# Attention into an MLP on one core: a two-chunk first load, another order of jobs among the first tiles, and one pair of row copies on another engine

## The chip, the cores and the metric

The kernel runs on one core of a Trainium2 chip. The metric is the device time of one execution in microseconds (us), as a median of several runs. TensorE does matrix products, VectorE (DVE) and ScalarE (ACT) the elementwise work, GpSimd (POOL) and SyncE (SP) mostly issue DMAs here. SBUF is the memory on the core, and PSUM holds the results of TensorE in banks.

## The reference

Attention with a sigmoid in the place of the softmax, for 8 batches of 12 heads, then a two-layer MLP with a silu over all 3584 tokens. Inputs and output are float32.

```python
batch, n_heads, seq, head_dim = (8, 12, 448, 64)
scale = 1.0 / np.sqrt(q.shape[-1])
scores = scale * np.matmul(q, k.transpose(0, 1, 3, 2)) - np.log(S)
attn = 1.0 / (1.0 + np.exp(-scores))
attn_out = np.matmul(attn, v).astype(np.float32)
x = np.ascontiguousarray(attn_out.transpose(0, 2, 1, 3)).reshape(B * S, H * D)
# n_tokens, d_model, d_ff = (3584, 768, 2048)
h = x @ w_in
g = h * (1.0 / (1.0 + np.exp(-h)))
return (g @ w_out).astype(np.float32)
```

## The kernel before, in words

The 96 pairs of batch and head are taken in 24 quads of four heads, three quads to a batch. A quad has its 448 rows in seven chunks of 64, and a tile is one chunk of k of one quad: `scores` (L169) multiplies it with q (four matmuls, L178, into `psc`, of which there are two), and ScalarE takes the sigmoid of 896 columns into `attnT` (L185). `values` (L195) multiplies `attnT` with v (L209, into `pav`), and VectorE scales the sum into `xT` (L225), two copies for a quad. `ptr`, `pav`, `ph`, `pw` and `po` share four PSUM banks (`ps_1`).

q and k have to be transposed first. For quads 0 to 5 TensorE does this against an identity (`pe_transpose`, L139, 14 matmuls for q or k at L147), and VectorE copies the result, in two pieces of 512 and 384 columns, to `kT` or `qT` (L154). For quads 6 and up (`dma_transpose`, L158) an engine first brings the rows into another order (the "row copies", L162, `kr` and `qr`; L137 where ScalarE does it), and then SP issues a DMA that transposes (L163). `rows_of_quad` (L646) calls that, and after q it makes GpSimd wait for the transpose and then issues the next loads; behind q of quad 6 these are v of quad 6, k and q of quad 8, v of quad 7, then k and q of quad 9.

The order on every engine is the order in which the program is written; nothing is rescheduled. It has two stages that matter here.

The first 24 tiles (three quads of batch 0 and three tiles of batch 1) are written out one after another. Behind the scores of tile n stand the jobs that a table `behind` (L690) gives: transposes of later quads, rounds of `values`, or dummy products that only keep TensorE busy (`keep_busy(n, short)`, L131: n of 512 columns, `short` of 128). `unread` (L172) puts dummy products of 128 columns ahead of a tile's scores, in its own `psc`. k of quad 0 is loaded in two pieces (L596 and L597), of which the first has `FIRST` chunks. Only that first piece is transposed ahead of tile 0.

Then the MLP begins. For batches 0 and 1 `h_unit` (L238) makes one of 16 parts of h with six matmuls (L244, into `ph`), one for each pair of heads; pairs 0 to 3 come from quads 0 and 1, pairs 4 and 5 from quad 2. ScalarE takes the sigmoid (`tsig`, L256) and VectorE multiplies into `gTr` (L257), after which the bank is free. All of this is one long generator (`all_moe`, L559), each step of which stands for one matmul and gives its length in ns. Bursts of two tiles (L735) are set between stretches of its steps: one for each `PACE` = 1600 ns up to tile 42, then a stretch of 13500 ns, then bursts spread so that the steps up to `h_at` last until the batches' end. Two parts of h (`early`, L525) can be begun ahead of the stretches, and their steps there aren't counted.

Row copies of quads 6, 7 and 8 stand in `rows_at` (L524), by the number of the part of h after which they come, and ScalarE does them. Those of later quads stand in a list `later`; `rows_if_any` (L656) takes one behind each burst, and VectorE does it. Later stages (output products `po` at L465, and the h of later batches) are not changed.

Of the kernel before, what the change touches and what calls it, by code (L numbers as in the profile page):

```python
# [18 lines left out]
def kernel(  # L19
# [16 lines left out]
    NCH = S // HP  # L36
# [3 lines left out]
    NCC = DMODEL // P  # L40
    NFC = DFF // P
# [44 lines left out]
                rows_in(name, g)[:, :, c0 * D : c1 * D],  # L86
            )

    FIRST, SPLIT = 1, 4

    def load_first_q():
        room = cpool.tile([P, NHC * NO2 // 2], F32, tag="T2", name="qs")
# [76 lines left out]
    def scores(g, ch, unread=0):  # L169
        attnT[g, ch] = p12.tile([P, 2, S], F16, tag="attnT", name="attnT")  # L170
        psc = ps_sc.tile([P, 2, 512], F32, tag="pssc", name="psc")
        for _ in range(unread):  # L172
            nc.tensor.matmul(psc[:, 0, :P], dummy[:, :P], dummy[:, :P], start=True, stop=True)
        for half in range(2):
            own = slice(half * HP, (half + 1) * HP)
            for j in range(2):
                rows = slice(j * D, (j + 1) * D)
                nc.tensor.matmul(  # L178
                    psc[own, j, :S],
                    qkT["k", g][rows, ch, own],  # L180
                    qkT["q", g][rows, :, own],
                    start=True,
                    stop=True,
                )
        nc.scalar.activation(  # L185
            attnT[g, ch], psc[:, :, :S], AF.Sigmoid, bias=NEG_LOG_S, scale=QKSCALE
        )
# [50 lines left out]
    def h_unit(b, fc):  # L238
        nonlocal hold
        hold = b > 0 and fc == NFC - 1  # L240
        ph = ps_1.tile([P, 512], F32, tag="ps1", name="ph")
        for at, cc in enumerate(pairs):
            assert b in ready or at < 4
            nc.tensor.matmul(  # L244
                ph[:, :S],
                w_in_of[:, cc // NQ, cc % NQ, fc * P : (fc + 1) * P],
                xT[b][:, cc, :],
                start=(at == 0),
                stop=(at == NCC - 1),
            )  # L250
            if at < NCC - 1:
                yield 189
        if fc == NFC - 1:
            h_done.add(b)
        tsig = p3.tile([P, 2 * S], F16, tag="m1", name="tsig")[:, :S]
        nc.scalar.activation(tsig, ph[:, :S], AF.Sigmoid, bias=0.0, scale=ISX)  # L256
        nc.vector.tensor_mul(  # L257
            gTr[:, fc, (b % 2) * S : (b % 2) * S + S], ph[:, :S], tsig
        )
        yield 189  # L260
# [43 lines left out]
    def h_pair(m, tail):  # L304
# [56 lines left out]
        EARLY = NHC - 2  # L361
        behind = None
        yield from begin(0)
        for i in range(NHC):
            end = i == NHC - 1
            if not end:
                yield from begin(i + 1)
# [153 lines left out]
        yield 163  # L521


    rows_at = {14: (6, "k"), 16: (6, "q"), 18: (7, "k"), 21: (7, "q"), 27: (8, "k"), 30: (8, "q")}  # L524
    early = [h_unit(0, fc) for fc in range(2)]  # L525
    sums = w_sums()
    in_sums = w_in_sums()
# [57 lines left out]
    def stretch(ns):  # L585
        nonlocal done, due
        due += ns
        while done < due or hold:
            step_ns = next(stream, None)
            if step_ns is None:  # L590
                break
            done += step_ns
# [19 lines left out]
    units = [(g, ch) for g in range(NQB) for ch in range(NCH)]  # L612
# [30 lines left out]
    later = []  # L643
# [12 lines left out]
    def rows_if_any():  # L656
        if later:
            rows_of_quad(*later.pop(0), nc.vector.tensor_copy)

    def values_if_any():  # L660
        if not waiting:
            return 0
        g, begin, end = waiting.pop(0)
        rounds(g, end)
        return end - begin
# [10 lines left out]
    def transposes(g, name):  # L676
        pe_transpose(g, ((name, 0, 4), (name, 4, NCH)))
        if name == "q":
            after_transpose(g)
# [3 lines left out]
        if end == NCH:  # L683
            after_values(g)

    def begin(fc, steps):
        for _ in range(steps):
            next(early[fc])

    behind = {  # L690
        0: ((pe_transpose, 0, (("k", FIRST, 4),)),),
        1: ((pe_transpose, 0, (("k", 4, NCH),)), (after_transpose, 0)),
        2: ((keep_busy, 2),),
        3: ((transposes, 1, "k"),),
        4: ((transposes, 1, "q"),),
        5: ((keep_busy, 2),),
        6: ((keep_busy, 2),),
        7: ((keep_busy, 2),),
        8: ((transposes, 2, "k"),),
        9: ((transposes, 2, "q"),),  # L700
        10: ((rounds, 0, 2),),
# [1 line left out]
        12: ((rounds, 0, 7),),  # L703
        13: ((rounds, 1, 2),),
        14: ((rounds, 1, 4),),
        15: ((transposes, 3, "k"),),
        16: ((rounds, 1, 7),),
        17: ((transposes, 3, "q"),),
        18: ((rounds, 2, 3),),
        19: ((transposes, 4, "k"),),  # L710
        20: ((rounds, 2, 5),),
        21: ((transposes, 4, "q"),),
        22: ((rounds, 2, 7),),
        23: ((begin, 0, 3),),
    }
    for n in range(NT_B + 3):
        scores(*units[n], unread={0: 7, 1: 7, 2: 3}.get(n, 0))
        for do, *what in behind.get(n, ()):
            do(*what)

    PACE, BURST, ROUND, SPARE = 1600, 590, 200, 2400
    sets = 7 * NHC * 163
    h_at = [(2 * NFC * NCC - 3) * 189 + 3 * sets]
    for m in (1, 2):
        h_at.append(h_at[-1] + 7 * NHC * HCC * 189 + (3 + m % 2) * sets)
    AHEAD = 4
# [3 lines left out]
    for n in range(NT_B + 3, len(units), 2):  # L730
        burst = units[n : n + 2]
        if n == 2 * NT_B:
            values_if_any()
            stretch(13500)
        for u in burst:  # L735
            scores(*u)
        had = values_if_any()
        rows_if_any()
        for g, ch in burst:
            if ch == NCH - 3 and g >= 6 and g % 6 < 4 and g + 3 < NQB:  # L740
                later.extend(((g + 3, "k"), (g + 3, "q")))
            if ch == NCH - 1:
                waiting.extend(((g, 0, NCH),) if n < 2 * NT_B else ((g, 0, 4), (g, 4, NCH)))
        if n in (30, 32):
            transposes(5, "kq"[n // 2 - 15])
        if n < ends[0]:
            stretch(PACE)
            continue
        m = bisect.bisect(ends, n)
        if n + 2 == ends[m]:  # L750
            nc.scalar.activation(warm, warm, AF.Silu)
        dense = h_at[m - 1] - SPARE - done
        due = done
        stretch((dense + values_left * ROUND) / ((ends[m] - n) // 2) - had * ROUND)
        values_left -= had
        if n + 2 == ends[m]:
            while waiting:
                values_if_any()
                stretch(SPARE / 3)
            values_left = 2 * NT_B  # L760
            while 2 * m not in h_done:
                done += next(stream)
            due = done
            stretch(3000)
# [32 lines left out]
```

## Time and profile before

| | us |
|---|---|
| median of three runs | 368.06 |
| lowest, highest | 367.29, 368.47 |
| profiled execution | 367.27 |
| its span, first to last instruction | 365.5 |
| TensorE busy in it | 357.7 (98%) |
| VectorE, ScalarE, GpSimd busy | 263.4, 250.5, 63.1 |

The profile is one execution, and the views are of that one. A row of an order in time has its start and length in us, the engine, the line, the operation, what is written and read, and the count of instructions merged; in brackets the idle time ahead of it and what ended it. A row of a grouped view has the busy time in us and the mean in ns of one behind the bar. TensorE's matmuls overlap, so a row of one matmul is longer than its share of the time.

### The profile page before, as it was taken

The numbers are of one execution on the slowest core, as the hardware profiler recorded it, in microseconds if no ns is written. First come the engines' busy times: TensorE is split into PE (matmuls) and PEld (weight loads), VectorE is DVE, ScalarE is ACT, GpSimd is POOL, SyncE is SP. The second block draws the span as 40 slices with busy tenths as digits, with TensorE's granted clock in tenths as the row PEclk, the third lists the DMA queues.
The fourth block names the chain that finished last, engine by engine and source line by source line (L and its number), as shares of the span: only waits on it lengthen the run. The fifth ranks groups of instructions, "written<-read, shape, count | busy, mean of one in ns | idle before, by whom it ended". The sixth has DMA issues, their size and how long they took to land.

```text
span 365.5 us, 7663 instructions
## 1 busy us (share of the span) xinstructions
PE 357.7 (98%) x3027; PEld 181.0 (50%) x3027; DVE 263.4 (72%) x495; ACT 250.5 (69%) x364; POOL 63.1 (17%) x105
## 2 busy tenths in 40 slices
PE   7999999999999999999999999999999999999995
PEld 3554445444444555554444455554444455555662
DVE  2584779876888587877668677886867577778773
ACT  4998877797778677586677768658878756660000
POOL 8544300604241002002014001100100000000000
PEclk9999999999999999999999999999999999999999
DMA  8999999999999437307999653822844020003333
GB/s 131 198 205 205 205 204 187 168 160 163 202 158 211 91 89 102 50 0 141 153 194 166 142 112 56 108 40 47 169 78 112 17 70 0 3 0 88 86 86 86
DMA packets 65314, 42.78 MB, mean 117 GB/s; under 512 B 35968, under 2 KB 61824, under 8 KB 65280
## 3 DMA queue, kind: packets, MB, share of 16 engines
q0 software_dynamic: 26944, 22.58, 42.2%
q1 hardware_dynamic: 38112, 19.41, 25.7%
q8 instruction: 23, 0.38, 0.4%
q10 hardware_dynamic: 224, 0.33, 0.3%
q14 instruction: 11, 0.09, 0.1%
HBM read 45.61 MB, written 11.01 MB: 155 GB/s over the span
## 4 chain that ended last, share of the span: by engine, by line
PE 84%; issue 5%; ACT 4%; DMA 3%; DVE 2%; POOL 1%; ACTq 0%; POOLq 0%; DVEq 0%
PE po L465 36%; PE hy L320 11%; PE psc L178 10%; PE pav L209 8%; PE hz L320 7%; PE hx L320 7%; PE ph L244 5%; ACT attnT L185 4%; DMA kf<-in_k_dram 3%; DVE xs L273 1%; DVE xT L225 1%; DVE kT L154 0%; DVE osb L475 0%; POOL vf L84 0%; PE ptrk L147 0%
## 5 line engine op out<-in xcount | busy, mean ns | idle before, releaser
L185 ACT ACTIVATE attnT<-psc 128x896 f16<-128x896 f32 x168 | 144.3, 917 | 31.9 <-PE psc L178 31.3
L465 PEld LDWEIGHTS <-S 128*128 128x128 f16 x448 | 41.1, 98 | 36.4 <-issue 11.7
L178 PE MATMUL psc<-qT,kT 64*64 64x448 f16 x672 | 51.1, 363 | 1.1 <-ACT attnT L185 0.7
L475 DVE SCALAR_TENSOR_TENSOR osb<-po,osb 128x384 f32<-128x384 f32 x70 | 37.6, 554 | 19.4 <-PE po L465 18.8
L225 DVE TENSOR_SCALAR xT<-pav 128x448 f16<-128x448 f32 x45 | 26.1, 620 | 26.5 <-PE pav L209 26.4
L331 ACT ACTIVATE gTr<-u 128x448 f16<-128x448 f32 x48 | 27.6, 575 | 23.1 <-DVE u L344 19.1
L465 PE MATMUL po<-T,S 128*128 128x384 f16 x224 | 41.6, 327 | 0.0
L465 PE MATMUL po<-w_out_sb,S 128*128 128x384 f16 x224 | 41.5, 327 | 0.0
L320 PEld LDWEIGHTS <-w_in_sb 128*128 128x128 f16 x288 | 28.2, 98 | 26.4 <-issue 0.4
L209 PE MATMUL pav<-attnT,vf 64*64 64x448 f16 x672 | 41.0, 350 | 0.2
L465 PEld LDWEIGHTS <-gTr 128*128 128x128 f16 x304 | 28.0, 98 | 25.5 <-issue 8.5
L244 PE MATMUL ph<-xT,w_in_sb 128*128 128x448 f16 x192 | 38.9, 353 | 0.0
L465 PE MATMUL po<-w_out_sb,gTr 128*128 128x384 f16 x192 | 36.6, 327 | 0.0
L320 PE MATMUL hy<-xs,w_in_sb 128*128 128x448 f16 x144 | 35.1, 352 | 0.1
L320 PE MATMUL hx<-xT,w_in_sb 128*128 128x448 f16 x144 | 34.6, 352 | 0.0
L178 PEld LDWEIGHTS <-kT 64*64 64x64 f16 x672 | 16.0, 104 | 30.3 <-issue 27.1
L320 PEld LDWEIGHTS <-W 128*128 128x128 f16 x216 | 21.1, 98 | 19.6
L257 DVE TENSOR_TENSOR gTr<-ph,tsig 128x448 f16<-128x448 f32 x32 | 19.9, 623 | 11.0 <-ACT tsig L256 10.5
L84 POOL DMA_DIRECT2D vf<-in_v_dram x24 | 17.0, 713 | 61.2 <-PE pav L209 50.6
L244 PEld LDWEIGHTS <-w_in_sb 128*128 128x128 f16 x192 | 17.6, 98 | 19.1 <-issue 4.0
L475 DVE SCALAR_TENSOR_TENSOR osb<-po,m 128x384 f32<-128x384 f32 x42 | 23.0, 553 | 5.3 <-PE psc L178 2.0
L209 PEld LDWEIGHTS <-vf 64*64 64x64 f16 x672 | 20.3, 107 | 11.8 <-issue 2.0
(75 smaller groups left out, 416.8 us busy)
## 6 DMA issues: line engine op xcount, KB each, us to landing
out_dram<-osb SPq DMA_DIRECT2D x54, 192.0 KB, 3.0
vf<-in_v_dram POOLq DMA_DIRECT2D x24, 224.0 KB, 7.1
kf<-in_k_dram POOLq DMA_DIRECT2D x23, 224.0 KB, 5.8
qf<-in_q_dram POOLq DMA_DIRECT2D x23, 224.0 KB, 6.5
w_in_sb<-in_moe_w_in_dram POOLq DMA_DIRECT2D x8, 384.0 KB, 12.2
w_out_sb<-in_moe_w_out_dram POOLq DMA_DIRECT2D x4, 768.0 KB, 17.4
kT<-kr SPq DMA_TRANSPOSE x18, 4.6
qT<-qr SPq DMA_TRANSPOSE x18, 3.3
```

Source lines behind the costliest of these rows:

```text
L84: nc.gpsimd.dma_start(flat[name, g][:, :, c0:c1].rearrange("p j c d -> p j (c d)"), rows_in(name, g)[:, :, c0 * D : c1 * D],)
L178: nc.tensor.matmul(psc[own, j, :S], qkT["k", g][rows, ch, own], qkT["q", g][rows, :, own], start=True, stop=True,)
L185: nc.scalar.activation(attnT[g, ch], psc[:, :, :S], AF.Sigmoid, bias=NEG_LOG_S, scale=QKSCALE)
L209: nc.tensor.matmul(pav[half][j * D : (j + 1) * D, :S], flat["v", g][own, j, ch, :], at[own, j, :], start=(ch == 0), stop=(ch == NCH - 1),)
L225: nc.vector.tensor_scalar_mul(xT[b][:, half * NQ + iq, :], pav[half][:, :S], SX)
L244: nc.tensor.matmul(ph[:, :S], w_in_of[:, cc // NQ, cc % NQ, fc * P : (fc + 1) * P], xT[b][:, cc, :], start=(at == 0), stop=(at == NCC - 1),)
L257: nc.vector.tensor_mul(gTr[:, fc, (b % 2) * S : (b % 2) * S + S], ph[:, :S], tsig)
L273: nc.vector.tensor_sub(o, x, y)
L320: nc.tensor.matmul(ps, a[:, c, i * P : (i + 1) * P], bs(c), start=(first and c == 0), stop=(c == HCC - 1), skip_group_check=True,)
L331: nc.scalar.activation(gTr[:, side * NHC + i, odd * S : (odd + 1) * S], src, AF.Silu, scale=ISX)
L465: nc.tensor.matmul(po[:, :NO2], a[:, fc, :], w[:, fc, :], start=(fc == 0), stop=(fc == NHC - 1))
L475: nc.vector.scalar_tensor_tensor(out=o, in0=po, scalar=sign * scale, in1=x, op0=ALU.mult, op1=ALU.add)
```

## The change

- `FIRST` goes from 1 to 2: the first piece of k has two chunks, and so have the transposes and ScalarE's copy ahead of tile 0. Tile 1 needs no further transposes.
- The table `behind` is laid out anew: the rest of k of quad 0 comes behind tile 1 in two pieces, one dummy product stands behind tile 0, and tiles 2 and 5 to 7 have a long and a short dummy product instead of two long ones. The rounds of values and the transposes of quads 3 and 4 change places so that tile 17 has no job and the last round of quad 2 stands behind tile 23. `unread` is 7, 0, 5 for tiles 0, 1, 2 instead of 7, 7, 3.
- Eight steps of h (four of each of the first two parts, of pairs 0 to 3) come behind that, where there were three of the first part; `h_at` is set to match.
- The row copies of quad 8 leave `rows_at`; they go into `later` ahead of the burst of tile 42, so VectorE does them, k behind that burst and q behind the next.

```diff
-    FIRST, SPLIT = 1, 4
+    FIRST, SPLIT = 2, 4
...
-    rows_at = {14: (6, "k"), 16: (6, "q"), 18: (7, "k"), 21: (7, "q"), 27: (8, "k"), 30: (8, "q")}
+    rows_at = {14: (6, "k"), 16: (6, "q"), 18: (7, "k"), 21: (7, "q")}
...
-    def begin(fc, steps):
-        for _ in range(steps):
-            next(early[fc])
-
     behind = {
-        0: ((pe_transpose, 0, (("k", FIRST, 4),)),),
-        1: ((pe_transpose, 0, (("k", 4, NCH),)), (after_transpose, 0)),
-        2: ((keep_busy, 2),),
+        0: ((keep_busy, 1),),
+        1: ((pe_transpose, 0, (("k", FIRST, 4), ("k", 4, NCH))), (after_transpose, 0)),
+        2: ((keep_busy, 1, 1),),
         3: ((transposes, 1, "k"),),
         4: ((transposes, 1, "q"),),
-        5: ((keep_busy, 2),),
-        6: ((keep_busy, 2),),
-        7: ((keep_busy, 2),),
+        5: ((keep_busy, 1, 1),),
+        6: ((keep_busy, 1, 1),),
+        7: ((keep_busy, 1, 1),),
         8: ((transposes, 2, "k"),),
         9: ((transposes, 2, "q"),),
         10: ((rounds, 0, 2),),
...
         14: ((rounds, 1, 4),),
-        15: ((transposes, 3, "k"),),
-        16: ((rounds, 1, 7),),
-        17: ((transposes, 3, "q"),),
-        18: ((rounds, 2, 3),),
-        19: ((transposes, 4, "k"),),
-        20: ((rounds, 2, 5),),
-        21: ((transposes, 4, "q"),),
-        22: ((rounds, 2, 7),),
-        23: ((begin, 0, 3),),
+        15: ((rounds, 1, 7),),
+        16: ((transposes, 3, "k"),),
+        18: ((transposes, 3, "q"),),
+        19: ((rounds, 2, 3),),
+        20: ((transposes, 4, "k"),),
+        21: ((rounds, 2, 5),),
+        22: ((transposes, 4, "q"),),
+        23: ((rounds, 2, 7),),
     }
     for n in range(NT_B + 3):
-        scores(*units[n], unread={0: 7, 1: 7, 2: 3}.get(n, 0))
+        scores(*units[n], unread={0: 7, 2: 5}.get(n, 0))
         for do, *what in behind.get(n, ()):
             do(*what)
+    for unit in early:
+        for _ in range(4):
+            next(unit)
...
-    h_at = [(2 * NFC * NCC - 3) * 189 + 3 * sets]
+    h_at = [(2 * NFC * NCC - 8) * 189 + 3 * sets]
...
             stretch(13500)
+            later.extend(((8, "k"), (8, "q")))
         for u in burst:
             scores(*u)
```

## The prediction

> **What bounds the kernel now.** I read the busy shares first, then the stretches, then the orders in time of TensorE and ScalarE, since a share of 98% hides what kind of work fills it.
>
> ```profile
> PE 357.7 (98%) x3027; PEld 181.0 (50%) x3027; DVE 263.4 (72%) x495; ACT 250.5 (69%) x364; POOL 63.1 (17%) x105
> ```
> ```profile
> 10.00:15.00 5.00, 5.00 (x76) 2.28 (x72) 2.50 (x5) 5.00 (x7) 2.75 (x4) 1.00 1.25 201
> 60.00:80.00 20.00, 19.34 (x124) 9.14 (x121) 17.34 (x34) 16.31 (x26) 5.84 (x10) 1.00 1.21 170
> ```
>
> TensorE is the bound of the whole, so the time is its useful work plus what it wastes. In a row of stretches the columns after the length are PE, PEld, DVE, ACT, POOL, then the granted clock and the DMA share. From 10 to 15 us TensorE and ScalarE are both busy for all 5.00 us, yet part of TensorE's work there is dummy products. From 60 to 80 us 0.66 us is missing from TensorE. These are the two places that the change touches; the rest is dense and moves bodily. The first 29 us in TensorE's order in time (start, length, count at the end of the row):
>
> ```profile
> 1.46 3.25 PE L134 MATMUL pw<-dummy 128*128 128x512 f16 x10 [1.46 <-DVE warm L607]
> ...
> 5.27 0.22 PE L147 MATMUL ptrk<-ident,kf 128*64 128x128 f16 x2
> ...
> 6.32 0.38 PE L178 MATMUL psc<-qT,kT 64*64 64x448 f16 x4 [0.16 <-ACT qT L137]
> 7.01 0.36 PE L147 MATMUL ptrk<-ident,kf 128*64 128x128 f16 x6 [0.30 <-DMA kf<-in_k_dram]
> ...
> 8.02 0.38 PE L178 MATMUL psc<-qT,kT 64*64 64x448 f16 x4 [0.16 <-DVE kT L154]
> ...
> 11.40 0.38 PE L178 MATMUL psc<-qT,kT 64*64 64x448 f16 x4
> 11.71 0.61 PE L134 MATMUL pw<-dummy 128*128 128x512 f16 x2
> 12.25 0.38 PE L178 MATMUL psc<-qT,kT 64*64 64x448 f16 x4
> ...
> 14.78 0.38 PE L178 MATMUL psc<-qT,kT 64*64 64x448 f16 x4
> 15.09 0.58 PE L147 MATMUL ptrq<-ident,qf 128*64 128x128 f16 x14
> 15.60 0.38 PE L178 MATMUL psc<-qT,kT 64*64 64x448 f16 x4
> ...
> 25.58 0.56 PE L209 MATMUL pav<-attnT,vf 64*64 64x448 f16 x8
> 26.18 0.38 PE L178 MATMUL psc<-qT,kT 64*64 64x448 f16 x4
> 26.50 2.56 PE L244 MATMUL ph<-xT,w_in_sb 128*128 128x448 f16 x12
> 28.99 0.57 PE L178 MATMUL psc<-qT,kT 64*64 64x448 f16 x8
> ...
> 63.83 3.95 PE L244 MATMUL ph<-xT,w_in_sb 128*128 128x448 f16 x20
> ```
> ```profile
> 5.54 0.28 ACT L137 ACTIVATE kT<-ptrk 128x128 f16<-128x128 f32 x1 [0.63 <-PE ptrk L147]
> 5.71 0.48 ACT L137 ACTIVATE qT<-ptrq 128x384 f16<-128x384 f32 x1
> 6.75 0.92 ACT L185 ACTIVATE attnT<-psc 128x896 f16<-128x896 f32 x1 [0.56 <-PE psc L178]
> 8.46 19.30 ACT L185 ACTIVATE attnT<-psc 128x896 f16<-128x896 f32 x23 [0.79 <-PE psc L178]
> ...
> 29.54 1.72 ACT L185 ACTIVATE attnT<-psc 128x896 f16<-128x896 f32 x2
> ```
>
> Three things are to be seen. The sigmoid of tile 0 starts at 6.75, that of tile 1 only at 8.46: its scores (8.02) waited for chunk 1 of k. The 23 sigmoids that follow take 19.30 us, (19.30 - 0.92)/22 = 0.835 us from start to start, where two with nothing between them take 1.72 - 0.92 = 0.80; so TensorE, not ScalarE, sets part of the pace. A slot with two dummy products lasts 12.25 - 11.40 = 0.85 us, one with 14 transposes 15.60 - 14.78 = 0.82. And the twelve h matmuls at 26.50 take 2.56 us where (3.95 - 0.35)/19 = 0.19 us each (from the row of twenty) makes 2.44: 0.12 us is a hidden wait for the xT copies of quad 2.
>
> The second place, 67 to 74 us, TensorE and then ScalarE:
>
> ```profile
> 67.70 0.57 PE L178 MATMUL psc<-qT,kT 64*64 64x448 f16 x8
> 68.21 2.06 PE L244 MATMUL ph<-xT,w_in_sb 128*128 128x448 f16 x10
> 70.20 0.57 PE L178 MATMUL psc<-qT,kT 64*64 64x448 f16 x8
> 70.71 2.07 PE L244 MATMUL ph<-xT,w_in_sb 128*128 128x448 f16 x10
> 73.01 0.38 PE L178 MATMUL psc<-qT,kT 64*64 64x448 f16 x4 [0.24 <-ACT attnT L185]
> ...
> 74.13 0.36 PE L244 MATMUL ph<-xT,w_in_sb 128*128 128x448 f16 x1
> ```
> ```profile
> 71.20 0.95 ACT L137 ACTIVATE kr<-kf 128x896 f16<-128x896 f16 x1 [0.47 <-DMA kf<-in_k_dram]
> 72.06 1.71 ACT L185 ACTIVATE attnT<-psc 128x896 f16<-128x896 f32 x2
> ```
>
> The scores of 70.20 are ready for ScalarE at about 70.7, but the row copy of quad 8 stands before them, waits 0.47 us for its DMA and takes 0.95. So the sigmoids start at 72.06, and the next scores find no free psc. The h matmuls after that burst should start at 70.71 + 2.50 (the burst period, 70.20 - 67.70) = 73.21 and start at 74.13: **0.92 us** lost.
>
> **The change, part by part.** *Two chunks first.* The first landing brings 64 KB instead of 32, the second 160 instead of 192. I take no wait for it: k's two transposes ran at 5.27 behind q's, without one. Four transposes instead of two put back what follows by some 0.05 us, and ScalarE's copy grows from 128 to 256 columns: between 0.28 (128) and 0.48 (384) that is 0.38. Tile 0 so starts about 0.16 us later, at 6.92. Its bound is 0 to 0.5 later, the upper end if the landing is late.
>
> Tile 1 now needs nothing more: its scores follow one dummy product (0.31 + 0.31 us, as in the slot rows) at 7.11, in the other psc, and its sigmoid runs at 6.92 + 0.80 = 7.72 instead of 8.46. The rest of k (chunks 2 to 6) is transposed behind it, at 7.4, after the landing seen at 7.01; the copy of chunks 2 and 3 is 256 columns wide.
>
> ```profile
> L154 DVE CAST kT<-ptrk 128x384 f16<-128x384 f32 x7 | 3.9, 551 | 2.0 <-PE ptrk L147 2.0
> ...
> L154 DVE CAST kT<-ptrk 128x512 f16<-128x512 f32 x5 | 3.4, 690 | 4.6 <-PE ptrk L147 3.5 <-ACT attnT L185 1.1
> ...
> L162 DVE COPY kr<-kf 128x896 f16<-128x896 f16 x2 | 1.2, 616 | 0.0
> ```
>
> From 551 and 690 ns a 256-column copy is 0.42 us, done at about 8.2; tile 2's scores go at 8.25, its sigmoid at 8.69 (0.16 late against the pace), tile 3 at 9.49, tile 4 at 10.29. Then the pace meets a landing. In slot 4 the transposes of quad 1's q would start at 10.07, and that load is not there.
>
> ```profile
> L84 POOL DMA_DIRECT2D qf<-in_q_dram x1: 715/715/715, 4.0 to 4.0; - x1
> ...
> DMA to landing us min/median/max: 6.3/6.3/6.3
> ```
>
> It was issued at 4.01 and took 6.3: 10.3. The queue is full then (DMA share 1.25), so being earlier elsewhere does not bring it. Tile 5's scores then come at 10.92 and its sigmoid at 11.36, where 11.09 would have been possible.
>
> *One job a slot, thinner dummies.* A slot with one long and one short dummy product lasts about 0.85 - 0.17 = 0.68 us, so ScalarE's 0.80 rules. Each transpose slot (0.82) stands beside shorter ones, and the copies of VectorE (about 1.15 us a pair) get the free slot 17. So tile 23's sigmoid starts at 11.36 + 18 x 0.80 = 25.76; before, at 8.46 + 22 x 0.835 = 26.83. Its scores, last in TensorE's queue, move from 26.18 to 25.13, 1.05 us.
>
> *What moves behind tile 23.* The last eight matmuls of quad 2's values go there, from the slot before: 0.39 us more ahead of the h matmuls, which start at about 25.13 + 0.71 = 25.84 instead of 26.50. That is **0.66 us** gained. Eight early h matmuls of pairs that are ready take 8 x 0.19 = 1.5 us and cover VectorE's two xT copies (1.15), so the hidden **0.12** goes too. They are work brought forward, worth nothing in themselves: every later burst has five more h matmuls before it. Bursts stay where they were (0.1 us later), with more work done.
>
> *Quad 8 by VectorE.* ScalarE loses 2 x 0.95 us of copies, and the 0.92 us of stall goes. VectorE gains two copies of 0.62 us, behind the bursts near 67.8 and 70.3. Each waits for its landing, and behind it in VectorE's order stand the multiplications that empty ph, of which there are at most four banks.
>
> ```profile
> 66.53 4.66 DMA kf<-in_k_dram
> ```
> ```profile
> L84 POOL DMA_DIRECT2D qf<-in_q_dram x1: 723/723/723, 67.2 to 67.2; - x1
> ...
> DMA to landing us min/median/max: 7.5/7.5/7.5
> ```
>
> k lands at 71.2, and I take that unchanged, since the loads follow a transpose that ends with a full DMA queue. VectorE arrives at about 69.5 and waits 1.7 us; the next multiplication ends at 72.4, and TensorE needs that bank at 73.4: covered by 1.0 us. q landed at 67.21 + 7.5 = 74.7, 3.5 us after k, though issued 0.7 us behind it; 224 KB at the 170 GB/s of the stretch from 60 to 80 us are 1.35 us, and by that it lands at 72.5, which I take for most executions. VectorE comes to that copy at 73.9. Landed by then, it costs nothing: the bank wanted at 76.4 is free at 75.5. At 74.7 the copy ends 0.9 us late, and TensorE waits some 0.15 us for a bank at the second output product and 0.5 at the pair of banks for the next values: 0.65 lost of the 0.92. SP's transpose of k is issued about as before, that of q earlier; GpSimd's loads of quad 11 behind it only gain.
>
> The Trainium skill ("TensorE: Matmul & The Clock Gate", Architectural detail) has ScalarE and VectorE as strict first-in, first-out queues. The row of 71.20 agrees: sigmoids ready at 70.7 waited behind a copy that waited for a DMA. By that rule the change moves the wait to another queue rather than ending it, which is the first rival.
>
> **Sum.** 0.66 + 0.12 + 0.92 = 1.70 us. The profiled execution took 367.27 us (span 365.5 and 1.8 around it), 0.8 below the median of 368.06; so 365.6 by its own time, and 366.4 by the median, which I give. From the unknowns: 0.3 more if quad 1's q lands earlier, 0.5 less if the first piece lands late.
>
> **Rivals.**
> *VectorE's queue pays* (0.24): q of quad 8 lands near 74.7 as in the trace. The gain is 1.05 us: 367.0. For it: the row. Against: the waits of ph have spare banks.
> *The start gives little* (0.10): tile 1 comes early, but waits at landings or at ps1 banks among slots 16 to 22 eat it. Left: 0.92 + 0.12, 367.0.
> *VectorE's queue pays more than it saved* (0.08), slower: the same place, q landing later than it did. Beyond 74.7 each microsecond goes through to TensorE, so from about 75.8 the whole gain is lost and from 76.9 the kernel is over 1.1 us slower; at 77.5, 369.8. Against: that q would be 2 us later than in this trace, where it already took 7.5 against k's 4.7.
> *The clock falls* (0.05), slower: the first ten dummies have 3968 columns in 3.25 us, 0.82 ns each; the row of twenty has 0.44. With fewer dummies the slow rate could come back in slots 5 to 15: 0.68 us becomes 1.26, 0.46 over the pace, eleven times: 371.4. It takes six such slots to be slower than before. Against: 1.00 granted in the stretch from 10 to 15, and no gap in a new slot over 0.2 us. The same page of the Trainium skill (Part 1) says that the gate closes after an idle window of some 3.4 us; no trace here has one.
> The forecast has what is left, 0.53.
>
> **How the numbers follow.** 0.3% of 368.06 is 1.1 us, about what a measurement of this kernel can tell from none. The forecast (gain 1.70, its own range 365.6 to 367.1 with the runs' scatter of 0.8 below the median) is faster in nine of ten of its cases; the first two rivals, 1.05 each, lie just at the line, a third of them faster. Faster: 0.53 x 0.9 + 0.34 x 0.33 = 0.59; slower 0.13; within it 0.28. The range takes in the forecast with the scatter below, 365.4, and both middle rivals with scatter above, 368.1.
>
> **What would show it.** Right: the first sigmoid near 6.9 and no gap before the second; starts 0.80 apart from tile 5; the first h matmul near 25.8; no psc gap near 73; VectorE's two row copies with their waits. Wrong: a gap of TensorE before h or values matmuls at 74 to 80 released by VectorE; a granted clock under 1.00 before 30 us; tile 0 later than 7.3.

## The result, and the profile after

The changed kernel takes 366.64 us (median of six runs, 366.32 to 366.80) where the kernel before takes 367.97 on the same chip (367.21 to 368.57): a ratio of 0.9964, 95% interval 0.9949 to 0.9979, so 1.33 us less. Forecast were 366.4 and a gain of 1.70. On another chip (below) the same two kernels stood at 0.9978 (0.9969 to 0.9987), 0.80 us apart. The two profiled executions differ by only 0.68 us (367.27 and 366.59; spans 365.5 and 364.8), and that of before was one of its shortest. The gain is there, but it is not made up as forecast.

The busy times, from the page of the profile, then TensorE's order in time over the first tiles:

```profile
PE 358.0 (98%) x3023; PEld 181.5 (50%) x3023; DVE 264.0 (72%) x497; ACT 248.3 (68%) x362; POOL 63.7 (17%) x105
```
```profile
5.03 0.64 PE L147 MATMUL ptrq<-ident,qf 128*64 128x128 f16 x8
5.45 0.43 PE L147 MATMUL ptrk<-ident,kf 128*64 128x128 f16 x4
...
6.99 0.39 PE L178 MATMUL psc<-qT,kT 64*64 64x448 f16 x4
...
7.63 0.38 PE L178 MATMUL psc<-qT,kT 64*64 64x448 f16 x4
...
21.51 0.38 PE L178 MATMUL psc<-qT,kT 64*64 64x448 f16 x4 [0.41 <-ACT attnT L185]
...
25.79 0.55 PE L209 MATMUL pav<-attnT,vf 64*64 64x448 f16 x8
26.27 3.39 PE L244 MATMUL ph<-xT,w_in_sb 128*128 128x448 f16 x17
```

ScalarE beside it:

```profile
5.92 0.38 ACT L137 ACTIVATE kT<-ptrk 128x256 f16<-128x256 f32 x1 [1.02 <-PE ptrk L147]
6.24 0.49 ACT L137 ACTIVATE qT<-ptrq 128x384 f16<-128x384 f32 x1
7.43 19.70 ACT L185 ACTIVATE attnT<-psc 128x896 f16<-128x896 f32 x24 [0.70 <-PE psc L178]
```

The 24 sigmoids run without a gap between tiles 0 and 1. TensorE waits for ScalarE in the empty slot 17 (21.51), so ScalarE is now the bound over most of that stage: (19.70 - 0.92)/23 = 0.82 us from start to start, where 0.80 was forecast. But tile 0's sigmoid starts at 7.43, not at 6.92. From the first eight transposes of q to the next row it is 5.45 - 5.03 = 0.42 us, and 5.27 - 5.03 = 0.24 before: TensorE ran at little more than half its rate here. The trace's record of the granted clock has full speed from 7.04 us on in this execution, and from 4.33 us on in that of before; an execution with full speed only after 5.5 us has a "late clock" in what follows. The h matmuls start at 26.27, 0.23 earlier than before and not 0.66. They no longer wait: (3.39 - 0.35)/16 = 0.19.

The next stretch is where the forecast failed. Around the values of quad 4, TensorE before, then after, then VectorE after, then ScalarE before and after:

```profile
44.65 0.57 PE L178 MATMUL psc<-qT,kT 64*64 64x448 f16 x8
45.05 1.49 PE L209 MATMUL pav<-attnT,vf 64*64 64x448 f16 x28
46.48 1.69 PE L244 MATMUL ph<-xT,w_in_sb 128*128 128x448 f16 x8
48.09 0.57 PE L178 MATMUL psc<-qT,kT 64*64 64x448 f16 x8
```
```profile
45.38 0.57 PE L178 MATMUL psc<-qT,kT 64*64 64x448 f16 x8
45.78 0.35 PE L209 MATMUL pav<-attnT,vf 64*64 64x448 f16 x2
46.38 1.51 PE L209 MATMUL pav<-attnT,vf 64*64 64x448 f16 x26 [0.24 <-DVE gTr L257]
47.82 1.69 PE L244 MATMUL ph<-xT,w_in_sb 128*128 128x448 f16 x8
49.44 0.57 PE L178 MATMUL psc<-qT,kT 64*64 64x448 f16 x8
```
```profile
45.70 0.62 DVE L257 TENSOR_TENSOR gTr<-ph,tsig 128x448 f16<-128x448 f32 x1 [1.41 <-ACT tsig L256]
```
```profile
41.75 1.24 ACT L256 ACTIVATE tsig<-ph 128x448 f16<-128x448 f32 x2
42.88 1.72 ACT L185 ACTIVATE attnT<-psc 128x896 f16<-128x896 f32 x2
44.48 0.56 ACT L256 ACTIVATE tsig<-ph 128x448 f16<-128x448 f32 x1
```
```profile
42.48 0.55 ACT L256 ACTIVATE tsig<-ph 128x448 f16<-128x448 f32 x1
43.51 1.73 ACT L185 ACTIVATE attnT<-psc 128x896 f16<-128x896 f32 x2 [0.47 <-PE psc L178]
45.12 0.99 ACT L256 ACTIVATE tsig<-ph 128x448 f16<-128x448 f32 x2
```

From burst to burst it is 48.09 - 44.65 = 3.44 us before and 49.44 - 45.38 = 4.06 after, with the same matmuls: 0.62 lost. Values need two banks, and the second is freed only by the multiplication that ends at 46.32. That multiplication waited for `tsig`, which stood behind two sigmoids of a burst on ScalarE. A part of h has six matmuls, and its `tsig` is written behind the sixth. By the program, 54 h matmuls stand ahead of the burst of tile 34 in the kernel before, which is nine whole parts, and 59 in the changed one, which is one short of ten. So before, two `tsig` stood ahead of that burst's sigmoids (41.75) and one behind (44.48); now one stands ahead (42.48) and two behind (45.12), so their banks are still taken when the values come with the next burst. By the count of matmuls a further part has begun in a third bank then, and one of the four is left. At the values of quad 3 it is 37.61 - 34.03 = 3.58 us from burst to burst after and 36.88 - 33.43 = 3.45 before: another 0.13. That the five matmuls shift the bursts against the parts of h, and that this causes both waits, is called the phase theory below.

Then the second place, TensorE and VectorE after:

```profile
69.10 0.57 PE L178 MATMUL psc<-qT,kT 64*64 64x448 f16 x8
69.61 1.88 PE L244 MATMUL ph<-xT,w_in_sb 128*128 128x448 f16 x9
71.41 0.57 PE L178 MATMUL psc<-qT,kT 64*64 64x448 f16 x8
...
73.72 0.57 PE L178 MATMUL psc<-qT,kT 64*64 64x448 f16 x8
```
```profile
71.03 0.62 DVE L162 COPY kr<-kf 128x896 f16<-128x896 f16 x1 [0.25 <-DMA kf<-in_k_dram]
...
73.87 0.61 DVE L162 COPY qr<-qf 128x896 f16<-128x896 f16 x1
```

Both bursts follow after 2.31 us, a burst and nine h matmuls, with no wait: the 0.92 us is back whole. VectorE waits 0.25 us for k, and not at all for q.

### The profile page after: what moved, and what is told of

It reads as the page before. It is cut to its first block, busy times and chain, and to the rows that moved or that the text cites. A ratio compares the mean times of both kernels' runs of the same rounds, so it can differ in the third digit from the quotient of the medians.

```text
span 364.8 us, 7652 instructions
## 1 busy us (share of the span) xinstructions
PE 358.0 (98%) x3023; PEld 181.5 (50%) x3023; DVE 264.0 (72%) x497; ACT 248.3 (68%) x362; POOL 63.7 (17%) x105
## 4 chain that ended last, share of the span: by engine, by line
PE 91%; ACT 4%; DVE 2%; DMA 1%; issue 1%; DVEq 0%
PE po L465 36%; PE hy L320 11%; PE psc L178 10%; PE ph L244 9%; PE pav L209 8%; PE hz L320 7%; PE hx L320 7%; ACT attnT L185 4%; DMA qs<-in_q_dram 1%; DVE xs L273 1%; PE ptrq L147 1%; PE ptrk L147 0%; DVE osb L475 0%; PE psc L173 0%; DVE xT L225 0%
## 5 line engine op out<-in xcount | busy, mean ns | idle before, releaser
L649 POOL COPY seen<-qT 1x1 f16<-1x1 f16 x15 | 3.9, 257 | 127.7 <-DMA qT<-qr 127.7
```

What stands on the lines that cost most here:

```text
L649: nc.gpsimd.tensor_copy(seen, qkT["q", g][:1, NCH - 1, P - 1 :])
```

## The experiments

There are ten runs in three groups, each group beside the kernel before on its chip (367.21, 367.22 and 366.99). The times expected in the first group were reckoned from 367.97 for the kernel before. It took 367.21 there, so differences and ratios are to be compared, not the times themselves.

**Start alone.** The changed kernel with the row copies back:

```diff
-    rows_at = {14: (6, "k"), 16: (6, "q"), 18: (7, "k"), 21: (7, "q")}
+    rows_at = {14: (6, "k"), 16: (6, "q"), 18: (7, "k"), 21: (7, "q"), 27: (8, "k"), 30: (8, "q")}
...
-            later.extend(((8, "k"), (8, "q")))
```

> The changed kernel with quad 8's row copies back with ScalarE, behind parts 27 and 30 of h. Prediction's sum: the start alone brings 0.66 + 0.12, so 0.8 below the kernel before, 367.2. Phase theory (the five h matmuls brought forward set the values of quads 3 and 4 at a moment when the last multiplication has not yet freed its bank; 0.15 + 0.6 us lost between the bursts of tiles 28 and 38): next to nothing is left of the start, 0.0 to 0.3 below before, 367.7 to 368.0, and the trace shows the two waits again, while the wait near 73 us is back.

Measured: 367.22, ratio 0.9994 (0.9983 to 1.0006). TensorE of this run:

```profile
46.11 1.51 PE L209 MATMUL pav<-attnT,vf 64*64 64x448 f16 x26 [0.24 <-DVE gTr L257]
...
74.00 0.38 PE L178 MATMUL psc<-qT,kT 64*64 64x448 f16 x4 [0.48 <-ACT attnT L185]
```

That is level with the kernel before, and the interval, from 0.6 us less to 0.2 more, excludes the 0.8 of the prediction's sum. By itself the new start brings nothing that can be measured: what it saves goes at the values, as the phase theory says.

**Copies alone.** The kernel before with the two copies moved:

```diff
-    rows_at = {... 27: (8, "k"), 30: (8, "q")}
+    rows_at = {14: (6, "k"), 16: (6, "q"), 18: (7, "k"), 21: (7, "q")}
...
             stretch(13500)
+            later.extend(((8, "k"), (8, "q")))
```

> The kernel before with nothing changed but quad 8's row copies, done by VectorE behind the bursts of tiles 42 and 44. Prediction's sum: 0.9 below before, 367.05, with no wait of TensorE at 73. Rival (VectorE's queue pays): the copy of k is reached a part of h earlier than in the changed kernel and waits longer; 0.3 to 0.6 of the 0.9 comes back as waits for ph banks, 367.4 to 367.7.

Measured: 367.05, ratio 0.9996 (0.9982 to 1.001). VectorE, then TensorE:

```profile
72.34 0.62 DVE L162 COPY kr<-kf 128x896 f16<-128x896 f16 x1 [3.03 <-DMA kf<-in_k_dram]
```
```profile
73.54 2.43 PE L244 MATMUL ph<-xT,w_in_sb 128*128 128x448 f16 x12 [0.28 <-DVE gTr L257]
76.67 1.46 PE L465 MATMUL po<-w_out_sb,gTr 128*128 128x384 f16 x8 [0.69 <-DVE gTr L257]
```

That is 0.16 us less than before, and the interval, from 0.7 less to 0.4 more, excludes the 0.9 of the prediction's sum. The rival holds. VectorE comes to the copy 3.03 us ahead of the landing, the multiplications stand behind it, and TensorE runs out of banks, first for h and then for the first output product: 0.28 + 0.69 us. (k was issued at 66.7 and took 5.6 us in this execution, where the eleven other profiles have 4.2 to 4.7. The profiled execution, 369.12, was the longest of twelve; a further wait in it, at 104 us, has to do with a later copy.)

**Phase back.** The changed kernel, with the bursts where they were in the order of h:

```diff
-    stretch(PACE)
+    stretch(PACE - 5 * 189)
     for n in range(NT_B + 3, len(units), 2):
```

> The changed kernel with the first stretch five steps (945 ns) shorter, so that every burst stands again where it stood in the order of h matmuls before the change. Phase theory: the waits at the values of quads 3 and 4 (0.75 us) go, 365.9; but the copy of quad 8's k is reached some 1.7 us earlier and its landing is where it was, so VectorE's wait may cost up to 0.9 near 72 us, 365.9 to 366.8. Rival (the waits come from the start itself, from ScalarE or VectorE being late, not from the phase): the waits stay and the time is that of the changed kernel, 366.6.

Measured: 366.90, ratio 0.9993 (0.9977 to 1.0008), 0.31 less than before. That misses both: the phase theory had 1.2 to 2.1 less, the rival 1.3. In the trace the waits at the values are gone (the 28 values stand in one row again, 1.49 us from 44.55), and VectorE's has come, at the upper end of what was allowed for it, 0.19 + 0.70 us:

```profile
71.76 0.62 DVE L162 COPY kr<-kf 128x896 f16<-128x896 f16 x1 [2.15 <-DMA kf<-in_k_dram]
```
```profile
72.96 2.43 PE L244 MATMUL ph<-xT,w_in_sb 128*128 128x448 f16 x12 [0.19 <-DVE gTr L257]
76.09 1.14 PE L465 MATMUL po<-w_out_sb,gTr 128*128 128x384 f16 x6 [0.70 <-DVE gTr L257]
```

**Phase back, copies a burst later.** As the last, and:

```diff
-            later.extend(((8, "k"), (8, "q")))
+        if n == 2 * NT_B + 2:
+            later.extend(((8, "k"), (8, "q")))
         for u in burst:
             scores(*u)
```

> As the one before, and quad 8's row copies one burst later (behind tiles 44 and 46), so that VectorE reaches them at about the moment of the changed kernel. Phase theory: both waits gone, 0.75 below the changed kernel, 365.9. Rival: 366.6.

Measured: 365.93, ratio 0.9965 (0.9953 to 0.9977). TensorE at quad 4's values, then VectorE's two copies:

```profile
44.14 0.57 PE L178 MATMUL psc<-qT,kT 64*64 64x448 f16 x8
44.55 1.49 PE L209 MATMUL pav<-attnT,vf 64*64 64x448 f16 x28
```
```profile
72.44 0.61 DVE L162 COPY kr<-kf 128x896 f16<-128x896 f16 x1
...
74.50 0.60 DVE L162 COPY qr<-qf 128x896 f16<-128x896 f16 x1
```

No wait is left at the values, and neither copy waits for its landing. With the run before it, this separates the two effects: the phase costs at 45 us, the copies' place at 72. The ratio is that of the changed kernel on the first chip (0.9964), so a gain over that kernel needs the two side by side.

**The changed kernel and this version side by side**, on a chip with before at 367.22. The first is the change, unaltered; the second is the version just shown.

> The changed kernel itself, beside the others on this chip. Its ratio to the kernel before should be that of its first runs, 0.996; and the version with the phase set back and the copies a burst later (last of this group) should be 0.75 us faster than it by the phase theory, the same by the rival (the waits at the values are made up for later, or the two chips differ).

> The phase set back and quad 8's copies a burst later, as run above, here on the same chip as the changed kernel: 0.75 us below it by the phase theory.

Measured: 366.42 (0.9978, 0.9969 to 0.9987) and 365.94 (0.9959, 0.9945 to 0.9972): 0.48 apart where 0.75 were expected. All five times of the second (365.56 to 366.10) lie below all eleven of the first (366.23 to 367.02). In the profiles TensorE's burst of tile 48 is 0.88 us earlier in the second (76.27 against 77.15), 0.14 of it from the start; why the medians show less is open. In the first, q landed late:

```profile
71.19 0.62 DVE L162 COPY kr<-kf 128x896 f16<-128x896 f16 x1 [0.60 <-DMA kf<-in_k_dram]
...
74.80 0.62 DVE L162 COPY qr<-qf 128x896 f16<-128x896 f16 x1 [0.86 <-DMA qf<-in_q_dram]
```

VectorE waited twice, TensorE not at all. In the second, too, q's copy waited 0.40 us and TensorE didn't. The second had its clock up early (5.19 us), as the execution of before that I worked from; ScalarE and TensorE:

```profile
6.90 19.91 ACT L185 ACTIVATE attnT<-psc 128x896 f16<-128x896 f32 x24 [0.48 <-PE psc L178]
```
```profile
7.11 0.38 PE L178 MATMUL psc<-qT,kT 64*64 64x448 f16 x4
...
8.24 0.38 PE L178 MATMUL psc<-qT,kT 64*64 64x448 f16 x4
...
10.37 0.58 PE L147 MATMUL ptrq<-ident,qf 128*64 128x128 f16 x14 [0.23 <-DMA qf<-in_q_dram]
10.88 0.38 PE L178 MATMUL psc<-qT,kT 64*64 64x448 f16 x4
...
25.95 2.44 PE L244 MATMUL ph<-xT,w_in_sb 128*128 128x448 f16 x12
```

Forecast for these rows were 6.92, 7.11, 8.25, 10.3 (the landing), 10.92 and 25.84.

**Long dummies again** in that version, behind tiles 2, 5, 6 and 7 (each `keep_busy, 1, 1` back to `keep_busy, 2`):

> The last of this group with two long dummy products again behind tiles 2, 5, 6 and 7. If TensorE's slots of 0.85 us set the pace there, tile 10's sigmoid comes at 15.7 instead of 15.4 and the kernel is 0.3 us slower than the last of this group; if the pace is ScalarE's alone, or if the clock needs the dummies, it is the same or faster.

Measured: 366.34, 0.40 more than the version without. ScalarE's row is to be read against the changed kernel's, which starts at the same time (7.43) and has the same jobs but for the dummies:

```profile
7.42 19.92 ACT L185 ACTIVATE attnT<-psc 128x896 f16<-128x896 f32 x24 [0.69 <-PE psc L178]
```

19.92 - 19.70 = 0.22 us of it is seen in the row; the rest is within the intervals. The longer dummies cost pace, and with the thin ones the clock did not fall: 1.00 was granted from 10 to 30 us in the changed kernel's profile, and every scores row of the first 24 tiles from 7.63 on has its 0.38 us.

**One chunk first again** in that version, with slots 0 and 1 as before:

```diff
-    FIRST, SPLIT = 2, 4
+    FIRST, SPLIT = 1, 4
...
-        0: ((keep_busy, 1),),
-        1: ((pe_transpose, 0, (("k", FIRST, 4), ("k", 4, NCH))), (after_transpose, 0)),
+        0: ((pe_transpose, 0, (("k", FIRST, 4),)),),
+        1: ((pe_transpose, 0, (("k", 4, NCH),)), (after_transpose, 0)),
...
-        scores(*units[n], unread={0: 7, 2: 5}.get(n, 0))
+        scores(*units[n], unread={0: 7, 1: 7, 2: 3}.get(n, 0))
```

> The last of this group with the first piece of k one chunk again, and the jobs of slots 0 and 1 as before the change. If tile 1's wait is what the first piece removes, tile 2's sigmoid comes at 9.33 instead of 8.99 and all later tiles 0.3 us later: 0.3 slower than the last of this group. Rival: the wait for quad 1's q (lands at 10.3 to 10.5) takes up that difference, and it is the same.

Measured: 366.25, 0.31 more than the version with two. The 23 sigmoids from tile 1 on end at 8.40 + 18.80 = 27.20 here, at 6.90 + 19.91 = 26.81 with two chunks: 0.39. In this execution the rest of k landed at 6.9, as late as in that of before; how much is left where it lands earlier, this run doesn't show.

```profile
8.40 18.80 ACT L185 ACTIVATE attnT<-psc 128x896 f16<-128x896 f32 x23 [0.74 <-PE psc L178]
```

**Phase alone**, in the kernel before:

```diff
-    stretch(PACE)
+    stretch(PACE + 5 * 189)
```

> The kernel before with nothing changed but the first stretch, longer by five steps (945 ns), so that every burst stands five h matmuls later in their order, as in the changed kernel. Phase theory: the waits of 0.14 us at the values of quad 3 and 0.6 at those of quad 4 appear in it as well, with everything else as before: 0.75 slower than before. Rival (the waits need the new order of the first tiles): no such waits, the same as before.

Measured: 367.85, ratio 1.0025 (1.0013 to 1.0037), 0.86 slower than before (366.99).

```profile
45.82 0.36 PE L209 MATMUL pav<-attnT,vf 64*64 64x448 f16 x2
46.42 1.51 PE L209 MATMUL pav<-attnT,vf 64*64 64x448 f16 x26 [0.24 <-DVE gTr L257]
```

The same wait at the same matmul, in a kernel with none of the other edits. The phase theory is shown; of the 0.86, its two waits are 0.75.

**Quad 1's q a slot later**, in the version with the phase back:

```diff
-        4: ((transposes, 1, "q"),),
-        5: ((keep_busy, 1, 1),),
+        4: ((keep_busy, 1, 1),),
+        5: ((transposes, 1, "q"),),
```

> The version with the phase back and the copies later, and in it the transposes of quad 1's q behind tile 5 instead of tile 4, changed about with that slot's dummies. Where the clock is granted early, TensorE waits 0.2 to 0.3 us there for the landing; where late, not. So the wait should be gone from the trace, and the time 0 to 0.3 below that version's (ratio to before 0.996 or 0.9955); more than 0.3 would mean that the wait counts in every execution.

Measured: 365.95, ratio 0.9964 (0.9953 to 0.9976): nothing gained. The wait for the landing is gone and another has come, since tile 7 needs that q and now waits for VectorE's copies of it:

```profile
12.63 0.38 PE L178 MATMUL psc<-qT,kT 64*64 64x448 f16 x4 [0.39 <-DVE qT L154]
```

## Why the prediction was right, and where it was not

*The start* was right in its working and too large in its size. With the clock up early, every step came within about 0.1 us, the wait for quad 1's q among them. But the 0.66 was reckoned against one execution of before, and its 26.50 for the h matmuls varies. Two other profiles have the old start, the copies alone (late clock) and the phase alone (early clock):

```profile
26.48 2.56 PE L244 MATMUL ph<-xT,w_in_sb 128*128 128x448 f16 x12
```
```profile
26.19 3.51 PE L244 MATMUL ph<-xT,w_in_sb 128*128 128x448 f16 x17
```

In both the rest of k landed at 6.5 to 6.6, where the execution that I worked from had it at 7.0 and TensorE waiting 0.30 us for it. The six profiles with the new start begin h between 25.95 (early clock) and 26.27 (the latest clock). So the 0.55 us between 26.50 and 25.95 is in part that late landing: with an early clock in both and the load in time, 26.19 - 25.95 = 0.24 is left, and between the averages, 26.39 and 26.07, it is 0.32. About half of the 0.66 was there. The clock adds its own scatter, and I took tile 0's 6.32 us from the execution where it came earliest; "tile 0 later than 7.3" was one of my signs of being wrong, and the changed kernel's profile has it. The page "TensorE: Matmul & The Clock Gate" of the Trainium skill says (Part 1) that the gate's window runs freely, so that the same kernel has a different number of slow matmuls from run to run. The rows of these runs agree (0.41 to 0.64 us for the same eight transposes).

*The hidden 0.12 us* before the h matmuls went, as forecast.

*"Bursts stay where they were, with more work done"* is the step that failed. I counted the five matmuls as worth nothing in themselves. They move the end of each part of h against the bursts, and a part whose last matmul slips behind a burst's scores gets its `tsig` only behind the tiles' sigmoids. Values coming next want its bank. This costs 0.13 + 0.62 us, about as much as I had forecast for the whole start; the run with the start alone stands at 0.9994, and the shift alone makes the old kernel 0.86 slower.

*Quad 8's copies* brought back the 0.92 us, but for a reason that I had only half. The cover I had worked out (1.0 us for k) rests on when VectorE gets there. The burst came at 69.10 instead of 67.8, moved by the waits of the failed step and the late clock, and so the copies met their landings. Where the burst comes at about 67.2 to 67.7 (the copies alone, and the phase back), VectorE waits 2 to 3 us and nearly all of the gain is lost. The larger gap, 0.70 us, stands at the first output product: VectorE works without a break from k's landing on, has not caught up by then, and comes to that multiplication only at 75.4 or 76.0. For k I had looked only at the first multiplication behind the copy. The rival "VectorE's queue pays" is thus real, at k more than at q, and was avoided by the loss elsewhere. Its other case happened in a run of the changed kernel: q landed at 74.8, and VectorE had come to that copy at 73.9, as forecast. TensorE lost nothing, and its bursts were 1.1 us behind the forecast (68.92 for 67.8), so that it wanted the banks later. Nor was 72.5 the usual landing of q: in the twelve profiles it came between 72.8 and 75.3, 1.1 to 3.8 us behind k, where I had taken 1.35. Most of the load came as fast as I had taken it, and one late part of it set the landing (last section).

*The sum* by what the runs showed: for the profiled pair, 0.23 + 0.12 - 0.75 + 0.92 = 0.52 us. TensorE's burst of tile 48 stands at 77.34 against 77.81 before, 0.47 earlier. It is still 0.47 at 208 us and 0.54 at the last output products, and the rest of the 0.68 comes later still; the change touches none of that. The second chip's profile of the changed kernel, against the same one of before, gives 0.41 + 0.12 - 0.75 + 0.92 = 0.70; the medians there differ by 0.80. The first chip's 1.33 is above both; its interval reaches down to 0.77, and the scatter of the kernel before (1.36 us between its runs, 0.48 for the changed one) was not taken apart. So it was partly luck that 366.4 came near: the forecast gain was too large by the 0.75 lost at the values and by half of the start, and the median of the kernel before on that chip lay higher than its profile.

*The clock rival* did not happen: the clock stayed at 1.00 in slots 5 to 15, and longer dummies made the kernel slower. *The start gives little* happened in effect, but neither at the landings nor in slots 16 to 22.

## What to carry to other kernels

Work brought forward is not free when two orders are woven together: it moves every later meeting of the two, and each place where a shared bank changes hands has to be looked at again. A copy that waits for a DMA belongs at a place that its engine reaches at about the time of the landing or after it: waits of up to 0.86 us cost TensorE nothing here, waits of 2 to 3 us nearly the whole gain. That place moves with everything ahead of it, so bursts that come earlier can break it, as with the phase back. When two edits are worth nothing singly and 1 us together, their places in time are tied, and setting each right by itself (here one shorter stretch and one burst later) brings 0.48 us more, 365.94 against 366.42. And a gain reckoned against one execution takes over that execution's late loads.

## What the runs showed of the hardware

TensorE came up to its full rate at moments between 4.33 and 7.04 us in the twelve profiled executions, though its work up to 5 us is the same in all of them. With the new start, the price was up to 0.5 us at tile 0 (sigmoids from 7.43 instead of 6.90), of which some 0.3 was left after 24 tiles (26.27 instead of 25.95). And a load can land almost two microseconds later behind its neighbour, with the same loads in line: quad 8's q landed 1.8 us after k in one run of the changed kernel (71.0 and 72.8) and 3.6 us after it in the other (71.2 and 74.8). The trace counts sixteen completions for that load. In the other run fifteen of them had come by 72.80 and the last at 74.78; in the profile of before it was fifteen by 72.62 and the last at 74.75. So one sixteenth of the load made it late.
